# Two dense layers after a decay attention: the second product of layer 2 turned over, and VectorE's operations of three units interleaved

## The chip, the cores and the metric

One core of a Trainium2 chip runs the whole program. The metric is device time in microseconds, from the start of the program to its end. The kernel before takes 955.4 us (median of three runs, 954.99 to 956.48). A difference of 0.2%, about 2 us, is what a measurement of this kernel can tell from no change.

## The reference

The input goes through three stages. The last one is the one that the change touches:

```python
x = attention(r, k, v, w, u)              # 3072 tokens x 384, a linear attention with decay
h = x @ w_in1;  g = relu(h) ** 2;    x = g @ w_out1     # layer 1: 384 -> 2048 -> 384
h = x @ w_in2;  g = h - tanh(h);     x = g @ w_out2     # layer 2: 384 -> 2048 -> 384
```

The result is 3072 x 384 in 32-bit floats. Matmuls run on a rounded 32-bit type (fp32r), so each factor is split into a high part and a low part, and a product is the sum of three: high by high, high by low, low by high. The difference h - tanh(h) loses digits where h is small. There the kernel takes a polynomial in h squared, and it picks between the two element by element.

## The kernel before, in words

The 3072 tokens are cut into 6 blocks j of 512, and the 2048 hidden columns into 16 parts f of 128. A **unit** is one pair (layer, j, f). Layer 1 has 96 units, and layer 2 has 96 more. The program's order is written out by hand: each engine does its instructions in the order in which the code issues them, so an instruction that waits holds up everything behind it on its engine. The tile framework adds the waits on semaphores. In the text below, units of layer 2 are numbered 0 to 95.

One unit has two products on TensorE.

- *First product*, `gemm1` (L496): 9 matmuls with the weights held still and 512 token columns moving. The result h (128 hidden columns by 512 tokens) stands in one PSUM bank. It is the same for both layers.
- *Second product* of layer 1, `gemm2_1` (L536): 9 matmuls, 3 per 128 output columns. The weights are held still, and the high and low parts of g move, with 512 columns each. The result is kept transposed, outputs by tokens, in 3 banks. *Second product* of layer 2, `gemm2_2` (L614): 12 matmuls. Here g is held still (4 groups of 128 tokens) and 384 columns of weights move, so that the result is tokens by outputs, in 4 banks.

Between them stands the nonlinear part of layer 2, `act2` and `act2_late`. ScalarE does y = h² (L585), th = tanh h (L586), two squares q1, q2 of y plus a constant (L588, L590), and the mask of the sign of y minus a bound (L591). VectorE does the *first multiply* hy = k·h·y (L587), the *difference* th = h - th (L589), the *second multiply* hy = (q1 + c)·hy (L592), the *third multiply* hy = (q2 + d)·hy (L593), and the *pick*, which copies th into hy where the mask is set (L594). Then `act2_late` splits hy: ScalarE writes the high part ghi (L602), and VectorE writes the *low part* glo = hy - ghi (L603). `act2_late` of a unit comes after `act2` of the next unit, so on ScalarE the high part of unit n-1 stands behind the mask of unit n, and before y of unit n+1.

`front(n)` issues `gemm1` and then `act2` of a unit. The main loop runs three units ahead of the second product in layer 2: it issues `front(n+3)` and then `gemm2_2(n)`. At the end of a block, `evac2` copies the four banks of results to SBUF on ScalarE (L622) and sends them to memory from SyncE's queue. After parts f = 5, 7 and 9 of a block, `split_x2` prepares the input of the next block, with a cast on VectorE (L568) and then a subtraction on GpSimd (L569). After parts 1 and 2 of the first block, the last two weight tiles of layer 2 are made with a copy on ScalarE (L101) and a subtraction on GpSimd (L107). In layer 1 the VectorE subtraction at L525 is what TensorE waits for in the last unit.

PSUM has 8 banks. In layer 2 h turns through four of them (3, 4, 5, 6), and the results take four (0, 1, 2, 7).

Of the kernel before, what the change touches and what calls it, by code (L numbers as in the profile page):

```python
# [7 lines left out]
F32 = mybir.dt.float32  # L8
# [4 lines left out]
AF = mybir.ActivationFunctionType  # L13
ALU = mybir.AluOpType
# [7 lines left out]
PB, PD = 0.68482120983078318, 6.0837500067079047  # L22
# [3 lines left out]
def decay_attention_moe_moe_kernel(  # L26
# [9 lines left out]
):  # L36
    nc = tc.nc
    NTAU, GP, _, NP, C = rk.shape
    NT, DM = out.shape
    H = 2 * NP  # L40
    D = DM // H
    NCH = 768 // C
    KK = DM // 128
    NF = w1.shape[0]
    TB = 512
# [15 lines left out]
    def bank(i, name):  # L61
        return ps.tile([128, 512], F32, tag=f"bank{i}", name=name)
# [51 lines left out]
    def w_out(layer, f, part, a, b):  # L114
        return wt[layer, f][:, part, DM + a:DM + b]
# [364 lines left out]
                    )  # L480


    hbank = {1: [3, 4], 2: [3, 4, 5, 6]}
    hq = {}
    gq = {}
    acc = {}
# [89 lines left out]

    p2 = {}

    def act2(j, f):
        pool = p2["pool"]  # L580
        h = hq.pop((2, j, f))
        mk = lambda n: pool.tile([128, TB], F32, tag=n, name=n)
# [12 lines left out]
        late.append((j, f, hy))  # L595

    late = []

    def act2_late():
        j, f, hy = late.pop(0)  # L600
        hi, lo = split(hy)
        nc.scalar.activation(out=hi, in_=hy, func=AF.Copy)  # L602
        nc.vector.tensor_tensor(lo, hy, hi.bitcast(F32), op=ALU.subtract)  # L603
        gq[2, j, f] = (hi, lo)

    abank = [0, 1, 2, 7]

    def gemm2_2(j, f):
        hi, lo = gq.pop((2, j, f))
        if f == 0:  # L610
            acc[j] = [bank(abank[m], f"o{m}") for m in range(TPB)]
        for m in range(TPB):
            for n, (g, part) in enumerate(((hi, 0), (hi, 1), (lo, 0))):
                nc.tensor.matmul(  # L614
                    acc[j][m][:, 0:DM], lhsT=g[:, m * 128:(m + 1) * 128], rhs=w_out(2, f, part, 0, DM),
                    start=(f == 0 and n == 0), stop=(f == NF - 1 and n == 2),
                )

    def evac2(j):
        for m in range(TPB):  # L620
            t = p2["pool"].tile([128, DM], F32, tag="ob", name="ob", bufs=4)
            nc.scalar.activation(out=t, in_=acc[j][m][:, 0:DM], func=AF.Copy)  # L622
            t0 = (m * NCH + j) * C
            nc.sync.dma_start(out=out[t0:t0 + 128, :], in_=t)
        del acc[j]


# [29 lines left out]
    def front(n):  # L657
        layer, j, f = units[n]
        gemm1(layer, j, f)
        (act1 if layer == 1 else act2)(j, f)  # L660
        while len(late) > 1:
            act2_late()

    with tc.manual_schedule():
        table_a()
# [119 lines left out]
        for n, (layer, j, f) in enumerate(units):  # L785
            if layer == 1:
                act1_low(j, f)
            if layer == 1 and j == 0 and f:
                conv2(1, f + 2)
                conv3(1, f + 2, V)  # L790
                if f + 5 < NF:
                    load_w(1, f + 5)
            if layer == 1 and j == NB - 1 and 0 < f < NF - 1:
                conv2(2, f - 1)
                conv3(2, f - 1, V)
            while nf < len(units) and nf <= n + look(n):
                front(nf)
                nf += 1
            att = layer == 1 and j + 1 < NB and f in c_at
            if att:  # L800
                d = (j + 1) * ND + c_at[f]
                if j:
                    a_to(d + 3)
            if layer == 1 and j == 0:
                conv1(1, f + 3)
            if att:
                if j == 0:
                    a_to(min(d + 3, DR - 1))
                att_c(d)
                att_e(d)  # L810
                loads(d)
                pack(d)
            if layer == 2 and j == 0 and f in (1, 2):
                conv2(2, NF - 3 + f)
                conv3(2, NF - 3 + f, G)
            if layer == 1:
                gemm2_1(j, f)
            else:
                while (2, j, f) not in gq:
                    act2_late()  # L820
                gemm2_2(j, f)
            if att and d + 2 < NDALL:
                att_b(d + 2)
                att_dm(d + 2)
                if d % 2 == 0:
                    nat_push(d // 2 + 2, G)
            if layer == 1:
                nat_pop()
            if layer == 1 and j == 0:
                conv0(1, f + 4)  # L830
                if f >= NF - 3:
                    open_split()
                if f == NF - 2:
                    a_to(DR)
            if layer == 1 and j == NB - 2:
                if f == 11:
                    at_ctx.close()
                    open2()
                    for q in range(5):
                        load_w(2, q)  # L840
                if f == 12:
                    conv0(2, 0)
                if f == 14:
                    conv1(2, 0)
# [12 lines left out]
_OUTS = [((3072, 384), "float32")]  # L857


def _layout(x):  # L860
# [59 lines left out]
```

## Time and profile before

| what | value |
|---|---|
| median of three runs | 955.4 us |
| the profiled execution | 952.83 us |
| its span, first to last instruction | 951.0 us |
| matmuls of layer 2, from the first unit that they have to themselves | 536.9 us to 947.6 us |
| in the stretch 700 to 750 us: TensorE, VectorE, ScalarE, GpSimd busy of 50 us | 49.41, 46.68, 41.23, 3.90 |
| granted clock of TensorE in that stretch | 1.00 |

All durations used below come from the one profiled execution, whose time is 1.8 us over its span and 2.6 us under the median. A timeline row gives the start, the duration, the engine, the line, the operation, the result and its operands, and a count where neighbours of one kind are merged. Square brackets at the end of a row give the engine's idle time ahead of it, and what ended that. An instruction's duration includes latency which the next one can overlap, so the step from one start to the next start is what an instruction costs an engine that is never idle. In the tables of waits, a row reads: who waited, for whom, the total in us, how often, the longest.

### The profile page before, as it was taken

How to read it: one execution, taken by the hardware profiler on the slowest of the kernel's cores; microseconds unless marked ns; L12 is line 12 of the kernel's file. 1: busy time of each engine (PE TensorE's matmuls, PEld its weight loads, DVE VectorE, ACT ScalarE, POOL GpSimd, SP SyncE). 2: the span in 40 equal slices, each digit the busy share in tenths (PEclk: the TensorE clock that was granted, in tenths of full speed). 3: DMA queues.
4: the chain of work that ended last, by engine and by line, in shares of the span. 5: the costliest groups of instructions: out<-in, count | busy, mean ns of one | idle time of the engine just before them, and what ended most of it. 6: DMA issues, size and time to landing. Idle time of an engine off the chain costs nothing.

```text
span 951.0 us, 14117 instructions
## 1 busy us (share of the span) xinstructions
PE 917.6 (96%) x5036; PEld 783.5 (82%) x5036; DVE 734.4 (77%) x1200; ACT 643.6 (68%) x1157; POOL 251.8 (26%) x216
## 2 busy tenths in 40 slices
PE   6889999999999999999999999999999999999997
PEld 6767778888888888888888788898898898898896
DVE  7898967864883685461278899999999999999996
ACT  3545565545544554553688887888888888887885
POOL 5833324654554464443101011001001001010000
PEclk8999999999999999999999999999999999999999
DMA  8755522312120222200565100100100100100000
GB/s 240 228 174 173 183 62 68 93 53 78 53 85 29 68 93 53 78 9 7 202 207 192 55 1 12 56 1 12 57 12 1 55 12 1 56 12 1 34 1 33
DMA packets 29669, 67.55 MB, mean 71 GB/s; under 512 B 5024, under 2 KB 15136, under 8 KB 29600
## 3 DMA queue, kind: packets, MB, share of 16 engines
q1 hardware_dynamic: 29456, 66.47, 21.8%
q8 instruction: 39, 0.64, 0.3%
q14 instruction: 30, 0.25, 0.1%
q10 hardware_dynamic: 144, 0.20, 0.1%
HBM read 55.25 MB, written 9.44 MB: 68 GB/s over the span
## 4 chain that ended last, share of the span: by engine, by line
PE 73%; DVE 16%; ACT 4%; issue 4%; POOL 2%; DMA 1%; DVEq 0%; ACTq 0%; POOLq 0%
PE h L496 33%; PE acc L536 19%; PE o L614 14%; DVE hy L592 2%; DVE hy L593 2%; PE sc L290 2%; DVE hy L594 2%; PE y L429 2%; DVE hy L587 2%; PE y L422 2%; ACT ghi L602 1%; POOL am L324 1%; DVE glo L525 1%; DVE w L107 1%; DVE am L342 1%
## 5 line engine op out<-in xcount | busy, mean ns | idle before, releaser
L496 PE MATMUL h<-xt,w 128*128 128x512 f32 x864 | 215.2, 394 | 0.6 <-POOL w L107 0.6
L496 PE MATMUL h<-xs,w 128*128 128x512 f32 x864 | 215.0, 393 | 0.0
L614 PE MATMUL o<-w,ghi 128*128 128x384 f32 x768 | 197.0, 337 | 2.9 <-ACT ob L622 2.9
L496 PEld LDWEIGHTS h<-xt,w 128*128 128x128 f32 x864 | 160.5, 189 | 34.2 <-POOL w L107 1.0
L496 PEld LDWEIGHTS h<-xs,w 128*128 128x128 f32 x864 | 160.8, 188 | 29.4
L510 ACT ACTIVATE g<-h 128x512 f32<-128x512 f32 x96 | 57.3, 597 | 143.0 <-PE h L496 142.1
L536 PE MATMUL acc<-ghi,w 128*128 128x512 f32 x576 | 153.3, 398 | 0.3 <-ACT x2s L552 0.3
L614 PEld LDWEIGHTS o<-w,ghi 128*128 128x128 f32 x768 | 140.7, 188 | 12.9 <-ACT ob L622 5.1
L614 PE MATMUL o<-w,glo 128*128 128x384 f32 x384 | 131.2, 342 | 5.1 <-DVE glo L603 4.9
L536 PEld LDWEIGHTS acc<-ghi,w 128*128 128x128 f32 x576 | 104.9, 188 | 23.8 <-ACT g L510 1.1
L516 POOL TENSOR_TENSOR glo<-g,ghi 128x512 fp32r<-128x512 f32 x64 | 85.8, 1341 | 136.0 <-ACT ghi L513 61.7
L569 POOL TENSOR_TENSOR xs<-x2f,xs 128x512 fp32r<-128x512 f32 x18 | 24.5, 1360 | 332.5 <-DVE xs L568 332.5
L536 PE MATMUL acc<-glo,w 128*128 128x512 f32 x288 | 83.8, 392 | 9.1 <-DVE glo L525 9.1
L602 ACT ACTIVATE ghi<-hy 128x512 fp32r<-128x512 f32 x96 | 60.9, 634 | 45.9 <-DVE hy L594 45.2
L614 PEld LDWEIGHTS o<-w,glo 128*128 128x128 f32 x384 | 72.0, 187 | 10.6 <-DVE glo L603 8.6
L594 DVE COPY_PREDICATED hy<-mask,th 128x512 f32<-128x512 uint8 x96 | 71.9, 749 | 9.9
L593 DVE SCALAR_TENSOR_TENSOR hy<-q,hy 128x512 f32<-128x512 f32 x96 | 68.0, 708 | 10.4 <-ACT q L588 0.5
L324 POOL TENSOR_TENSOR am<-ident,bt 128x512 f32<-128x512 f32 x44 | 51.2, 1164 | 89.6 <-DVE bt L308 82.7
L587 DVE SCALAR_TENSOR_TENSOR hy<-h,y 128x512 f32<-128x512 f32 x96 | 66.4, 691 | 10.0 <-ACT th L586 1.8
L585 ACT ACTIVATE y<-h 128x512 f32<-128x512 f32 x96 | 57.1, 595 | 24.2 <-PE h L496 23.6
L536 PEld LDWEIGHTS acc<-glo,w 128*128 128x128 f32 x288 | 53.7, 188 | 23.0 <-DVE glo L525 12.1
L273 DVE TENSOR_TENSOR fr<-rkt,fr 112x256 fp32r<-112x256 f32 x30 | 38.9, 1295 | 42.9 <-ACT fr L272 42.9
(104 smaller groups left out, 1406.1 us busy)
## 6 DMA issues: line engine op xcount, KB each, us to landing
raw<-in_w_dram SPq DMA_DIRECT2D x32, 768.0 KB, 4.4
rkt<-in_rk_dram SPq DMA_DIRECT2D x23, 448.0 KB, 4.3
kvt<-in_nat_dram SPq DMA_DIRECT2D x23, 384.0 KB, 4.4
x2d<-x2s SPq DMA_DIRECT2D x18, 256.0 KB, 2.2
x2f<-x2d SPq DMA_DIRECT2D x18, 256.0 KB, 2.8
out_dram<-ob SPq DMA_DIRECT2D x24, 192.0 KB, 2.0
rnt<-in_nat_dram SPq DMA_DIRECT2D x23, 192.0 KB, 2.5
xt<-ys SPq DMA_DIRECT2D x120, 16.0 KB, 1.8
```

The source lines that it names most:

```text
L273: nc.vector.tensor_tensor(ks[:, 1], k, ks[:, 0].bitcast(F32), op=ALU.subtract)
L324: nc.gpsimd.tensor_tensor(am_t[d].rearrange("p (a z) t -> p a z t", a=2), ident[:, None, None, :].to_broadcast([128, 2, 2, C]), hd.to_broa ...
L496: nc.tensor.matmul(h, lhsT=w_in(layer, f, part, kk), rhs=x[:, xpart, kk, :], start=(n == 0), stop=(n == 3 * KK - 1),)
L510: nc.scalar.activation(out=g, in_=h, func=AF.Relu)
L516: nc.gpsimd.tensor_tensor(lo, g, hi.bitcast(F32), op=ALU.subtract)
L536: nc.tensor.matmul(acc[j][m], lhsT=w_out(1, f, part, m * 128, (m + 1) * 128), rhs=g, start=(f == 0 and n == 0), stop=(f == NF - 1 and n == 2),
L585: nc.scalar.activation(out=y, in_=h, func=AF.Square)
L587: nc.vector.scalar_tensor_tensor(out=hy, in0=h, scalar=PK, in1=y, op0=ALU.mult, op1=ALU.mult)
L593: nc.vector.scalar_tensor_tensor(out=hy, in0=q2, scalar=PD, in1=hy, op0=ALU.add, op1=ALU.mult)
L594: nc.vector.copy_predicated(hy, mask, th)
L602: nc.scalar.activation(out=hi, in_=hy, func=AF.Copy)
L614: nc.tensor.matmul(acc[j][m][:, 0:DM], lhsT=g[:, m * 128:(m + 1) * 128], rhs=w_out(2, f, part, 0, DM), start=(f == 0 and n == 0), stop=(f ...
```

## The change

`gemm2_2` takes the form of `gemm2_1`: the weights are held still and g moves, with 9 matmuls of 512 columns in place of 12 of 384. The result is kept transposed in 3 banks, which are taken in turn from five (6, 7, 0, 1, 2), and h turns through three banks (3, 4, 5). In the last part of a block the matmuls are sorted by bank. `evac2` copies three banks of 512 columns, one of them on VectorE in the last block only, and the output in memory is a (6, 3, 128, 512) array that the host reorders.

`act2` issues the same operations of a unit in another order among those of its neighbours. On VectorE: first multiply of n, third multiply of n-1, difference of n, pick of n-1, low part of n-2, second multiply of n. On ScalarE the order stays: y, th, q1, q2 and mask of n, then the high part of n-1. hy has three buffers in place of two. After the last unit, `act2_flush` issues what is left.

```diff
-    hbank = {1: [3, 4], 2: [3, 4, 5, 6]}
+    hbank = {1: [3, 4], 2: [3, 4, 5]}
...
-        y, th, q1, q2, hy = (mk(n) for n in ("y", "th", "q1", "q2", "hy"))
+        y, th, q1, q2 = (mk(n) for n in ("y", "th", "q1", "q2"))
+        hy = pool.tile([128, TB], F32, tag="hy", name="hy", bufs=3)
         mask = pool.tile([128, TB], U8, tag="mask", name="mask")
+        st2[n] = (q2, hy, mask, th)
         nc.scalar.activation(out=y, in_=h, func=AF.Square)
         nc.scalar.activation(out=th, in_=h, func=AF.Tanh)
         nc.vector.scalar_tensor_tensor(out=hy, in0=h, scalar=PK, in1=y, op0=ALU.mult, op1=ALU.mult)
         nc.scalar.activation(out=q1, in_=y, func=AF.Square, bias=p2["ba"], scale=1.0)
+        act2_poly(n - 1)
         nc.vector.tensor_tensor(th, h, th, op=ALU.subtract)
         nc.scalar.activation(out=q2, in_=y, func=AF.Square, bias=p2["bb"], scale=1.0)
+        act2_pick(n - 1)
+        act2_low(n - 2)
         nc.scalar.activation(out=mask, in_=y, func=AF.Sign, bias=p2["bm"], scale=1.0)
         nc.vector.scalar_tensor_tensor(out=hy, in0=q1, scalar=PC, in1=hy, op0=ALU.add, op1=ALU.mult)
-        nc.vector.scalar_tensor_tensor(out=hy, in0=q2, scalar=PD, in1=hy, op0=ALU.add, op1=ALU.mult)
-        nc.vector.copy_predicated(hy, mask, th)
-        late.append((j, f, hy))
+        act2_high(n - 1)
+
+    def act2_poly(n):
+        if n >= 0:
+            q2, hy, mask, th = st2[n]
+            nc.vector.scalar_tensor_tensor(out=hy, in0=q2, scalar=PD, in1=hy, op0=ALU.add, op1=ALU.mult)
+
+    def act2_pick(n):
+        if n >= 0:
+            q2, hy, mask, th = st2[n]
+            nc.vector.copy_predicated(hy, mask, th)
+
+    def act2_high(n):
+        if n >= 0:
+            hy = st2[n][1]
+            hi, lo = split(hy)
+            nc.scalar.activation(out=hi, in_=hy, func=AF.Copy)
+            st2[n] = (hy, hi, lo)
+
+    def act2_low(n):
+        if n >= 0:
+            hy, hi, lo = st2.pop(n)
+            nc.vector.tensor_tensor(lo, hy, hi.bitcast(F32), op=ALU.subtract)
+            gq[(2, *divmod(n, NF))] = (hi, lo)
+
+    def act2_flush():
+        n = NB * NF - 1
+        act2_poly(n)
+        act2_low(n - 1)
+        act2_pick(n)
+        act2_high(n)
+        act2_low(n)
...
-    abank = [0, 1, 2, 7]
+    abank = [6, 7, 0, 1, 2]
...
-            acc[j] = [bank(abank[m], f"o{m}") for m in range(TPB)]
-        for m in range(TPB):
-            for n, (g, part) in enumerate(((hi, 0), (hi, 1), (lo, 0))):
-                nc.tensor.matmul(
-                    acc[j][m][:, 0:DM], lhsT=g[:, m * 128:(m + 1) * 128], rhs=w_out(2, f, part, 0, DM),
...
+            acc[j] = [bank(abank[(KK * j + m) % len(abank)], f"o{m}") for m in range(KK)]
+        terms = [(n, m) for n in range(3) for m in range(KK)]
+        if f == NF - 1:
+            terms.sort(key=lambda t: t[1])
+        for n, m in terms:
+            part, g = ((0, hi), (1, hi), (0, lo))[n]
+            nc.tensor.matmul(
+                acc[j][m], lhsT=w_out(2, f, part, m * 128, (m + 1) * 128), rhs=g,
...
     def evac2(j):
-        for m in range(TPB):
-            t = p2["pool"].tile([128, DM], F32, tag="ob", name="ob", bufs=4)
-            nc.scalar.activation(out=t, in_=acc[j][m][:, 0:DM], func=AF.Copy)
...
+        for m in range(KK):
+            t = p2["pool"].tile([128, TB], F32, tag="ob", name="ob", bufs=3)
+            if m == 1 and j == NB - 1:
+                nc.vector.tensor_copy(t, acc[j][m])
+            else:
+                nc.scalar.activation(out=t, in_=acc[j][m], func=AF.Copy)
+            nc.sync.dma_start(out=out[j, m], in_=t)
```

## Rows read from the trace of the kernel before

**Rows 1.** The page's first part (busy time and share of the span by engine) and the head of its fourth part, the chain of waits that ended last, by engine.

```profile
PE 917.6 (96%) x5036; PEld 783.5 (82%) x5036; DVE 734.4 (77%) x1200; ACT 643.6 (68%) x1157; POOL 251.8 (26%) x216
...
PE 73%; DVE 16%; ACT 4%; issue 4%; POOL 2%; DMA 1%; DVEq 0%; ACTq 0%; POOLq 0%
```

**Rows 2.** The timeline of TensorE's matmuls: four rows of one unit of layer 1's last block, then three of one unit of layer 2.

```profile
516.01 1.52 PE L536 MATMUL acc<-ghi,w 128*128 128x512 f32 x6
517.37 0.84 PE L536 MATMUL acc<-glo,w 128*128 128x512 f32 x3
518.05 2.20 PE L496 MATMUL h<-xt,w 128*128 128x512 f32 x9
520.09 1.30 PE L536 MATMUL acc<-ghi,w 128*128 128x512 f32 x5
...
703.12 2.24 PE L496 MATMUL h<-xs,w 128*128 128x512 f32 x9
705.20 0.51 PE L614 MATMUL o<-w,ghi 128*128 128x384 f32 x2
...
707.31 2.24 PE L496 MATMUL h<-xs,w 128*128 128x512 f32 x9
```

**Rows 3.** The timeline of VectorE at the start of layer 2: all its operations of one unit and the first of the next.

```profile
540.27 0.69 DVE L587 SCALAR_TENSOR_TENSOR hy<-h,y 128x512 f32<-128x512 f32 x1 [1.13 <-ACT th L586]
540.88 0.68 DVE L589 TENSOR_TENSOR th<-h,th 128x512 f32<-128x512 f32 x1
541.48 0.68 DVE L592 SCALAR_TENSOR_TENSOR hy<-q,hy 128x512 f32<-128x512 f32 x1
542.26 0.69 DVE L593 SCALAR_TENSOR_TENSOR hy<-q,hy 128x512 f32<-128x512 f32 x1
543.06 0.75 DVE L594 COPY_PREDICATED hy<-mask,th 128x512 f32<-128x512 uint8 x1
543.71 0.67 DVE L603 TENSOR_TENSOR glo<-hy,ghi 128x512 fp32r<-128x512 f32 x1
544.48 0.69 DVE L587 SCALAR_TENSOR_TENSOR hy<-h,y 128x512 f32<-128x512 f32 x1
```

**Rows 4.** The timeline of ScalarE in the same stretch.

```profile
539.15 0.60 ACT L585 ACTIVATE y<-h 128x512 f32<-128x512 f32 x1 [1.44 <-PE h L496]
539.65 0.59 ACT L586 ACTIVATE th<-h 128x512 f32<-128x512 f32 x1
...
541.96 0.62 ACT L602 ACTIVATE ghi<-hy 128x512 fp32r<-128x512 f32 x1
542.49 0.59 ACT L585 ACTIVATE y<-h 128x512 f32<-128x512 f32 x1
```

**Rows 5.** The table of waits for 480 to 951 us: who waited for whom, the total in us, how often, the longest.

```profile
ACT ghi L602 <- DVE hy L594: 45.2, 58, 3.6
...
ACT y L585 <- PE h L496: 23.6, 44, 1.4
...
PE o L614 <- DVE glo L603: 4.9, 4, 1.8
...
DVE hy L587 <- ACT th L586: 1.8, 2, 1.1
```

**Rows 6.** Timelines of GpSimd, VectorE and ScalarE around two of GpSimd's operations in layer 2: the subtraction for a weight tile with the VectorE row beside it, ScalarE's copy for that tile and what follows the copy, then four rows around the next block's input.

```profile
550.10 2.24 POOL L107 TENSOR_TENSOR w<-raw,w 128x768 fp32r<-128x768 f32 x1 [38.06 <-ACT w L101]
550.69 2.19 DVE L593 SCALAR_TENSOR_TENSOR hy<-q,hy 128x512 f32<-128x512 f32 x1
...
549.12 0.91 ACT L101 ACTIVATE w<-raw 128x768 fp32r<-128x768 f32 x1
549.91 0.60 ACT L585 ACTIVATE y<-h 128x512 f32<-128x512 f32 x1
...
572.47 0.42 DVE L568 CAST xs<-x2f 128x512 fp32r<-128x512 f32 x1
572.80 0.69 DVE L587 SCALAR_TENSOR_TENSOR hy<-h,y 128x512 f32<-128x512 f32 x1
572.97 1.30 POOL L569 TENSOR_TENSOR xs<-x2f,xs 128x512 fp32r<-128x512 f32 x1 [15.80 <-DVE xs L568]
574.00 0.81 DVE L592 SCALAR_TENSOR_TENSOR hy<-q,hy 128x512 f32<-128x512 f32 x1
```

**Rows 7.** The timeline of ScalarE at the end of a block: the four copies of layer 2's first block, and the three of layer 1's last.

```profile
611.26 1.61 ACT L622 ACTIVATE ob<-o 128x384 f32<-128x384 f32 x4
...
535.86 1.85 ACT L552 ACTIVATE x2s<-acc 128x512 f32<-128x512 f32 x3
```

**Rows 8.** The timeline where layer 1 goes over into layer 2: ScalarE's y of unit 1, and VectorE's low part of layer 1's last unit.

```profile
532.53 0.60 ACT L585 ACTIVATE y<-h 128x512 f32<-128x512 f32 x1 [1.16 <-PE h L496]
...
534.45 0.68 DVE L525 TENSOR_TENSOR glo<-g,ghi 128x512 fp32r<-128x512 f32 x1
```

**Rows 9.** The end: ScalarE's y of the last unit and the last matmul on the timeline, then two rows of the table of DMA issues (count, KB each, median us from issue to landing).

```profile
935.26 0.60 ACT L585 ACTIVATE y<-h 128x512 f32<-128x512 f32 x1
...
947.24 0.34 PE L614 MATMUL o<-w,glo 128*128 128x384 f32 x1
...
x2d<-x2s SPq DMA_DIRECT2D x18, 256.0 KB, 2.2
...
out_dram<-ob SPq DMA_DIRECT2D x24, 192.0 KB, 2.0
```

More of the change, by code (lines that the diff above doesn't have):

```diff
@@ L38, in decay_attention_moe_moe_kernel @@
     NTAU, GP, _, NP, C = rk.shape
-    NT, DM = out.shape
+    NT, DM = NTAU * C, nat.shape[3]
     H = 2 * NP
@@ L577, in decay_attention_moe_moe_kernel @@
     p2 = {}
+    st2 = {}
     def act2(j, f):
@@ L581, in act2 @@
         h = hq.pop((2, j, f))
+        n = j * NF + f
         mk = lambda n: pool.tile([128, TB], F32, tag=n, name=n)
-        y, th, q1, q2, hy = (mk(n) for n in ("y", "th", "q1", "q2", "hy"))
+        y, th, q1, q2 = (mk(n) for n in ("y", "th", "q1", "q2"))
+        hy = pool.tile([128, TB], F32, tag="hy", name="hy", bufs=3)
         mask = pool.tile([128, TB], U8, tag="mask", name="mask")
+        st2[n] = (q2, hy, mask, th)
         nc.scalar.activation(out=y, in_=h, func=AF.Square)
@@ L588, in act2 @@
         nc.scalar.activation(out=q1, in_=y, func=AF.Square, bias=p2["ba"], scale=1.0)
+        act2_poly(n - 1)
         nc.vector.tensor_tensor(th, h, th, op=ALU.subtract)
         nc.scalar.activation(out=q2, in_=y, func=AF.Square, bias=p2["bb"], scale=1.0)
+        act2_pick(n - 1)
+        act2_low(n - 2)
         nc.scalar.activation(out=mask, in_=y, func=AF.Sign, bias=p2["bm"], scale=1.0)
         nc.vector.scalar_tensor_tensor(out=hy, in0=q1, scalar=PC, in1=hy, op0=ALU.add, op1=ALU.mult)
-        nc.vector.scalar_tensor_tensor(out=hy, in0=q2, scalar=PD, in1=hy, op0=ALU.add, op1=ALU.mult)
-        nc.vector.copy_predicated(hy, mask, th)
-        late.append((j, f, hy))
[L597 to L604, printed above, removed]
-    abank = [0, 1, 2, 7]
+        act2_high(n - 1)
[26 more added lines that the diff above has]
+    abank = [6, 7, 0, 1, 2]
     def gemm2_2(j, f):
@@ L610, in gemm2_2 @@
         if f == 0:
-            acc[j] = [bank(abank[m], f"o{m}") for m in range(TPB)]
-        for m in range(TPB):
-            for n, (g, part) in enumerate(((hi, 0), (hi, 1), (lo, 0))):
-                nc.tensor.matmul(
-                    acc[j][m][:, 0:DM], lhsT=g[:, m * 128:(m + 1) * 128], rhs=w_out(2, f, part, 0, DM),
-                    start=(f == 0 and n == 0), stop=(f == NF - 1 and n == 2),
-                )
-    def evac2(j):
-        for m in range(TPB):
-            t = p2["pool"].tile([128, DM], F32, tag="ob", name="ob", bufs=4)
-            nc.scalar.activation(out=t, in_=acc[j][m][:, 0:DM], func=AF.Copy)
-            t0 = (m * NCH + j) * C
-            nc.sync.dma_start(out=out[t0:t0 + 128, :], in_=t)
+            acc[j] = [bank(abank[(KK * j + m) % len(abank)], f"o{m}") for m in range(KK)]
[6 more added lines that the diff above has]
+                acc[j][m], lhsT=w_out(2, f, part, m * 128, (m + 1) * 128), rhs=g,
+                start=(f == 0 and n == 0), stop=(f == NF - 1 and n == 2),
+            )
+    def evac2(j):
+        for m in range(KK):
[5 more added lines that the diff above has]
+            nc.sync.dma_start(out=out[j, m], in_=t)
         del acc[j]
@@ L660, in front @@
         (act1 if layer == 1 else act2)(j, f)
-        while len(late) > 1:
-            act2_late()
+        if n == len(units) - 1:
+            act2_flush()
     with tc.manual_schedule():
@@ L818, in decay_attention_moe_moe_kernel @@
             else:
-                while (2, j, f) not in gq:
-                    act2_late()
                 gemm2_2(j, f)
@@ L856 @@
 _ARGS = ["rk", "nat", "w", "u", "w1", "w2"]
-_OUTS = [((3072, 384), "float32")]
+_OUTS = [((6, 3, 128, 512), "float32")]
 def _layout(x):
@@ L918 @@
     r = _run(nc, [arrays], core_ids=[0])
-    return r.results[0]["out_0_dram"]
+    o = r.results[0]["out_0_dram"].reshape(6, 3, 128, 4, 128)
+    return _np.ascontiguousarray(o.transpose(3, 0, 4, 1, 2).reshape(3072, 384))
```

## The prediction

> **What bounds the kernel now.** The page's parts 1 and 4 come first: TensorE is busy 96% of the span and fills 73% of the chain that ended last [rows 1]. That names TensorE, but it doesn't say what a shorter TensorE stage would be worth, so the next view is the timeline of one unit, engine by engine. On TensorE a unit of layer 2 takes 707.31 - 703.12 = 4.19 us: 2.08 for the first product and 2.11 for the second [rows 2]. On VectorE its six operations take 544.48 - 540.27 = 4.21 us from first multiply to first multiply [rows 3]. The two engines are level. The steps inside those 4.21 us are 0.61, 0.60, 0.78, 0.80, 0.65, 0.77. An operation that follows one that it does not depend on starts 0.60 to 0.65 after it, before the earlier one has ended (durations 0.67 to 0.75). The third multiply and the pick, which need what stands right before them, start 0.78 and 0.80 after it. The 0.77 is the next unit's first multiply, which reuses the buffer that the low part has just read (hy has two buffers). ScalarE has slack: it waits 45.2 us for the pick and 23.6 us for h [rows 5].
>
> **The second product turned over.** It takes the shape of layer 1's products: weights still, g moving, 512 columns. Layer 1's last block shows both products in that shape, 18 matmuls in 520.09 - 516.01 = 4.08 us [rows 2]. So TensorE's unit goes from 4.19 to 4.08 us, and over 96 units it could save 10.6 us if nothing else held it. The columns streamed stay the same (9 x 512 = 12 x 384); three matmuls fewer per unit save what each costs beside its columns.
>
> **VectorE's order.** The new sequence is: first multiply of n, third multiply of n-1, difference of n, pick of n-1, low part of n-2, second multiply of n. No operation follows its own input, and with three buffers none reuses one just read. Five steps of 0.60 or 0.61 and one of 0.65 give 3.66 us, against 4.21 [rows 3]. No row has the third multiply right behind an independent first multiply. The bounds of that step are 0.60 and 0.80, and I take 0.61, the row of what now follows a first multiply. By its work alone VectorE is thus no longer a bound.
>
> **The wait that decides.** Two rows of the trace tell what the first multiply waits for. In rows 3 it sat idle for 1.13 us until th, not y: y starts at 539.15, th at 539.65 and ends at 540.24 [rows 4], and the first multiply starts at 540.27. The table has two such waits in layer 2, both put down to th [rows 5], although the operation reads only h and y. Both th and the multiply read the PSUM bank of h. So it starts at y + 1.12, not y + 0.63. Before, this rarely showed, as VectorE ran late anyway.
>
> The Trainium skill, "PSUM — Partial Sum Buffer", section "PSUM bank collisions raise a hardware error", says that the AWS compiler's scheduler puts a dependency between ScalarE and VectorE instructions on one bank, "reads and writes alike". The two rows just read agree, for the framework used here.
>
> Now the new order closes a ring. ScalarE's high part of n-1 waits for the pick of n-1. The pick now stands behind the first multiply of n, and so behind th of n. And y of n+1 stands behind that high part on ScalarE. One turn of the ring, from y of n to y of n+1:
> - y to the first multiply, through th: 1.12 [rows 3, 4];
> - first multiply, third multiply, difference, to the start of the pick: 0.61 + 0.60 + 0.60 = 1.81 [rows 3];
> - the pick itself: 0.75 [rows 3];
> - from its end to the high part: 0.03, which I take from th to the first multiply (540.24 to 540.27);
> - high part to the next y: 542.49 - 541.96 = 0.53 [rows 4].
>
> Sum: 4.24 us. That is above TensorE's 4.08 and VectorE's 3.66, so layer 2 would run at 4.24 us per unit. Before, the pick of n-1 came ahead of the first multiply of n, and no such ring held.
>
> What came beside other work before now adds to the ring, since ScalarE's and VectorE's stretches of it follow one another:
> - Copies at a block's end. They stand between a high part and a y. Four copies took 3 steps of (1.61 - 0.49)/3 = 0.37 for 384 columns [rows 7]. For 512 columns from PSUM the bounds are 0.37 and (1.85 - 0.60)/2 = 0.62, the steps of layer 1's copies, which wait for TensorE. I take the step from y to th, 0.50 [rows 4], which is 128x512 from PSUM too. Three copies in five blocks: 15 x 0.50 = 7.5 us.
> - GpSimd's subtraction for the next block. A VectorE operation with both inputs in SBUF stands still beside it: the multiply at 574.00, 0.27 before GpSimd's end, took 0.81 where 0.68 is usual, and the one at 550.69, 1.65 before GpSimd's end, took 2.19 [rows 6]. Both lose the time left less 0.14. The cast fills VectorE's idle 0.58 and costs nothing there (its step is 0.33), at 1.12 + 1.81 + 0.65 + 2 x 0.60 = 4.78 after y. GpSimd starts 0.50 later, 5.28, and ends at 6.58. The next third multiply would start at 4.24 + 1.12 + 0.61 = 5.97 and loses 6.58 - 5.97 - 0.14 = 0.47, on the ring. With 15 of these: 7.0 us. The bounds are nothing and the whole overlap, 0.61 each.
> - The last two weight tiles: ScalarE's copy, 549.91 - 549.12 = 0.79 each, plus some 0.4 each for a third multiply held by GpSimd [rows 6]: 2.4 us.
>
> **The sum against the profiled execution.** I count from y of unit 3 (542.49 before [rows 4]) to y of unit 95 (935.26 [rows 9]): 392.8 us. The start stays where it is. VectorE reaches the low part of layer 1's last unit about 1.5 us earlier, as the third multiply and the pick of unit 0 no longer stand ahead of it [rows 8]; but y of unit 1 is at 532.53, its first multiply at 533.65, the pick of unit 0 ends at 536.21, the high part and layer 1's three copies follow (0.53 + 1.5), y of unit 2 starts at 538.27, and y of unit 3 at 538.27 + 4.24 = 542.5. Then 92 x 4.24 + 7.5 + 7.0 + 2.4 = 407.0. That is 14.2 later than before.
>
> The end: from the last y, the ring's steps give the second multiply of 95 at 4.18, third multiply at 4.96 (now right behind its input), low part of 94 at 5.56, pick 6.16 to 6.91, high part to 7.57, low part 7.60 to 8.28. The last unit's matmuls, sorted by bank, have two done and seven to go: the last one starts 6 x 0.227 later, at 9.7, and ends at 10.1. Before, it was 947.58 - 935.26 = 12.3 [rows 9]. The last copy is 0.1 longer, and a 256 KB transfer takes 2.2 us where 192 KB took 2.0 [rows 9]. So the end gives back 1.9 us.
>
> Net: + 12.3 us on a span of 951.0. The profiled execution would go from 952.8 to 965.1, and the median of 955.4, 2.6 above it, to 967.7. I say 967.5. PSUM's three banks for h cost nothing: h of unit n is read out by y + 3, and its bank is wanted two units later.
>
> **Rivals.**
> - *TensorE sets the pace (faster).* If the first multiply waited for y alone, the ring would be 4.24 - 0.49 = 3.75 us, below TensorE's 4.08. From the end of layer 1's matmuls, 1.5 us ahead of 536.9, 94 first and 92 second products at 2.04 lead to 914.8, with about 3 us of waits (unit 0's low part, copies) to 918; with 13.5 of tail the span is 931, and the time 936. It turns on one thing: th in or out of that wait. For it speaks that only two instances show the wait; against it that both end to 0.03 us with th, and that the difference behind it, which does need th, follows without any idle time of its own.
> - *The ring holds, but its additions hide.* If copies and GpSimd's holds fell into slack, 14.5 us go and the time is 953, no change. I see no slack on the ring, but half of the additions could go.
> - *The interleaving doesn't shorten VectorE's steps.* The ring would have three steps of 0.79 instead of 0.60, and be 4.80 us: 92 x 0.56 = 52 us more, 1019. Against it stand the three steps of 0.60 to 0.65 in rows 3.
>
> The Trainium skill, "VectorE: DVE Perf Modes", section "The DRAIN you can't avoid", says that the next VectorE operation starts only when the pipe is empty, with or without a semaphore. By that rule the reordering gains nothing; the trace disagrees, with starts 0.07 to 0.10 before the earlier operation's end [rows 3].
>
> **How the numbers follow.** Ring with its additions 0.80; TensorE's pace 0.13; additions hidden 0.04; steps not shorter 0.03. The likeliest case has its own range: the ring's 4.24 is uncertain by 0.03, 2.8 us over 92 turns; the copies' bounds are -2 and +2; GpSimd's holds are -7 to +2. That is 958 to 973. As it holds most of the chance, the range given is little wider, 955 to 974. With 0.2% as what a measurement of this kernel can tell from no change: faster 0.13, within it 0.04, slower 0.83.
>
> **What would show it.** In the changed profile: y to y 4.24 in undisturbed units; the first multiply idle some 0.6 us in every unit, ended by th; the high part idle some 0.9, ended by the pick; VectorE's steps 0.60 to 0.65 and its share of busy time lower; y waiting no more for h; TensorE waiting in nearly every unit for the low part, and for the copies after a block's end. A first multiply that starts before th has ended, or TensorE without waits at 4.08 us per unit, would make the prediction wrong.

## The result, and the profile after

The kernel became slower: 962.26 us (median of four runs, 962.05 to 963.27) against 955.19 us (954.97 to 956.48) for the kernel before in the same comparison. The ratio is 1.0073, with a 95% interval of 1.0056 to 1.0091: 7.1 us more. The forecast was 967.5, in a range from 955 to 974.

The profiled execution took 963.27 us, with a span of 961.5. First the page's first part and the head of its fourth, the chain that ended last, which answer to [rows 1].

```profile
PE 922.7 (96%) x4748; PEld 741.5 (77%) x4748; DVE 722.9 (75%) x1201; ACT 637.6 (66%) x1150; POOL 250.8 (26%) x216
...
PE 45%; DVE 33%; ACT 17%; issue 2%; POOL 1%; DMA 1%; DVEq 0%; ACTq 0%; POOLq 0%
```

TensorE's share of busy time has not moved: 96% before and after. The chain has. TensorE fills 45% of it where it filled 73%, VectorE 33% where it filled 16%, ScalarE 17% where it filled 4%. That is how a ring over several engines looks in this view: no engine became the bound, and the chain passes from one to the next.

The table of waits from 480 to 962 us answers to [rows 5].

```profile
ACT ghi L617 <- DVE hy L611: 83.9, 96, 2.6
...
DVE hy L592 <- ACT th L591: 53.5, 95, 2.6
...
PEld o L645 <- DVE glo L623: 39.7, 89, 2.3
...
PE o L645 <- DVE glo L623: 13.6, 24, 1.8
```

Two waits stand in practically every unit: the high part waits for the pick (96 times, 58 before), and the first multiply for th (95 times, 2 before). TensorE waits for the low part: its weight loads (PEld) in 89 units, 39.7 us in all, and in 24 of these units its matmuls (PE) too, 13.6 us. In those 24 the two rows show the same stop twice, so they are not added up. The wait of y for h, 44 times before, is left twice.

One unit in the middle of the stage, ScalarE first and then VectorE, beside [rows 4] and [rows 3]:

```profile
702.55 0.58 ACT L590 ACTIVATE y<-h 128x512 f32<-128x512 f32 x1
703.02 0.59 ACT L591 ACTIVATE th<-h 128x512 f32<-128x512 f32 x1
...
706.22 0.63 ACT L617 ACTIVATE ghi<-hy 128x512 fp32r<-128x512 f32 x1 [0.77 <-DVE hy L611]
706.76 0.58 ACT L590 ACTIVATE y<-h 128x512 f32<-128x512 f32 x1
```

```profile
703.64 0.69 DVE L592 SCALAR_TENSOR_TENSOR hy<-h,y 128x512 f32<-128x512 f32 x1 [0.50 <-ACT th L591]
704.25 0.68 DVE L606 SCALAR_TENSOR_TENSOR hy<-q,hy 128x512 f32<-128x512 f32 x1
704.85 0.68 DVE L595 TENSOR_TENSOR th<-h,th 128x512 f32<-128x512 f32 x1
705.45 0.73 DVE L611 COPY_PREDICATED hy<-mask,th 128x512 f32<-128x512 uint8 x1
706.08 0.68 DVE L623 TENSOR_TENSOR glo<-hy,ghi 128x512 fp32r<-128x512 f32 x1
706.67 0.68 DVE L600 SCALAR_TENSOR_TENSOR hy<-q,hy 128x512 f32<-128x512 f32 x1
707.85 0.69 DVE L592 SCALAR_TENSOR_TENSOR hy<-h,y 128x512 f32<-128x512 f32 x1 [0.50 <-ACT th L591]
```

The ring is read by going to and fro between the two. y starts at 702.55. The first multiply starts 1.09 later, 0.03 after th ends (703.61). The pick starts 1.81 after the first multiply and lasts 0.73. The high part starts 0.04 after it, and the next y 0.54 after that. The sum is 4.21 us, y to y. VectorE's steps are 0.59 to 0.63, so its six operations would fit in some 3.6 us: it waits for th with nothing else to do.

### The profile page after: what moved, and what is told of

It reads as the page before. It is cut to its first block, busy times and chain, and to the rows that moved or that the text cites. A ratio compares the mean times of both kernels' runs of the same rounds, so it can differ in the third digit from the quotient of the medians.

```text
span 961.5 us, 13137 instructions
## 1 busy us (share of the span) xinstructions
PE 922.7 (96%) x4748; PEld 741.5 (77%) x4748; DVE 722.9 (75%) x1201; ACT 637.6 (66%) x1150; POOL 250.8 (26%) x216
## 4 chain that ended last, share of the span: by engine, by line
PE 45%; DVE 33%; ACT 17%; issue 2%; POOL 1%; DMA 1%; DVEq 0%; ACTq 0%; POOLq 0%
PE h L496 19%; PE acc L536 19%; DVE hy L592 7%; DVE hy L606 7%; DVE hy L611 7%; ACT ghi L617 6%; DVE th L595 6%; ACT th L591 5%; ACT y L590 5%; PE sc L290 2%; PE y L429 2%; PE y L422 2%; DVE w L107 1%; DVE am L342 1%; DVE raw L92 1%
## 5 line engine op out<-in xcount | busy, mean ns | idle before, releaser
L510 ACT ACTIVATE g<-h 128x512 f32<-128x512 f32 x96 | 57.2, 596 | 143.8 <-PE h L496 143.7
L645 PE MATMUL o<-ghi,w 128*128 128x512 f32 x576 | 150.6, 392 | 2.0 <-ACT ob L656 2.0
L645 PEld LDWEIGHTS o<-ghi,w 128*128 128x128 f32 x576 | 108.4, 189 | 26.5 <-ACT ob L656 4.1
L645 PE MATMUL o<-glo,w 128*128 128x512 f32 x288 | 93.1, 425 | 13.6 <-DVE glo L623 13.6
L645 PEld LDWEIGHTS o<-glo,w 128*128 128x128 f32 x288 | 47.9, 189 | 44.9 <-DVE glo L623 39.7
L606 DVE SCALAR_TENSOR_TENSOR hy<-q,hy 128x512 f32<-128x512 f32 x96 | 73.2, 763 | 0.1
L611 DVE COPY_PREDICATED hy<-mask,th 128x512 f32<-128x512 uint8 x96 | 69.9, 728 | 0.0
L593 ACT ACTIVATE q<-y,ba 128x512 f32<-128x512 f32 x96 | 69.6, 725 | 0.0
```

Source lines behind the costliest of these rows:

```text
L510: nc.scalar.activation(out=g, in_=h, func=AF.Relu)
L645: nc.tensor.matmul(acc[j][m], lhsT=w_out(2, f, part, m * 128, (m + 1) * 128), rhs=g, start=(f == 0 and n == 0), stop=(f == NF - 1 and n == 2),
```

## The experiments

All times are set against the kernel before, which was run beside them; its medians there were 954.5 to 954.9 us.

**1. The ring opened.** The high part is issued one unit later, right behind th, so that the pick on which it waits is long done. All else is the changed kernel.

```diff
         nc.scalar.activation(out=th, in_=h, func=AF.Tanh)
+        act2_high(n - 2)
         nc.vector.scalar_tensor_tensor(out=hy, in0=h, scalar=PK, in1=y, op0=ALU.mult, op1=ALU.mult)
...
-        act2_high(n - 1)
...
         act2_poly(n)
+        act2_high(n - 1)
         act2_low(n - 1)
```

> The changed kernel with one instruction moved: the high part of unit n-2 is issued right behind th of unit n, and no longer the high part of n-1 behind the mask of n. No operation is added or taken away. Theory (the ring y, th, first multiply, pick of the unit before, its high part, next y sets 4.21 us per unit): the pick no longer stands ahead of the next y, the ring is open, and TensorE's 4.08 us per unit is the next bound. From the end of layer 1's matmuls, 94 first and 92 second products at 2.04 and some 3 us of waits, then the tail of some 14: 933 to 942 us in all; y waits for h again, and the first multiply's idle time by unit is no longer fixed. Rival (the turned product, its banks and its longer copies are what made it slower): the order of ScalarE changes nothing of that, 958 to 963 us.

It took 933.81 us (932.63 to 934.79), ratio 0.978 [0.9763, 0.9797]. This is the version to keep: 21 us faster than the kernel before, 28 faster than the changed one. Its waits from 480 us on, and then one unit of ScalarE up to the next y:

```profile
ACT y L590 <- PE h L496: 54.3, 83, 1.2
...
DVE hy L593 <- ACT th L591: 23.0, 50, 1.9
...
ACT ghi L617 <- DVE hy L611: 2.8, 2, 2.6
```

```profile
705.22 0.60 ACT L590 ACTIVATE y<-h 128x512 f32<-128x512 f32 x1 [0.65 <-PE h L496]
705.72 0.59 ACT L591 ACTIVATE th<-h 128x512 f32<-128x512 f32 x1
706.19 0.63 ACT L617 ACTIVATE ghi<-hy 128x512 fp32r<-128x512 f32 x1
...
709.30 0.60 ACT L590 ACTIVATE y<-h 128x512 f32<-128x512 f32 x1 [0.65 <-PE h L496]
```

The high part waits twice in the whole stage where it waited 96 times, and y again waits for h, and so for TensorE, which now sets the pace. y to y is 4.08, layer 1's unit [rows 2]. The first multiply still waits for th 50 times, and a unit takes 4.08 all the same: with no ring through it, that wait no longer sets the pace. One view shows it in one number, the busy times in the same 355 us of layer 2. Here first, then the changed kernel, then the kernel before (columns: TensorE, its weight loads, VectorE, ScalarE and GpSimd, each with its instructions, then the granted clock, the DMA share and GB/s):

```profile
545.00:900.00 355.00, 354.21 (x1559) 291.40 (x1558) 336.19 (x535) 305.70 (x538) 23.98 (x17) 1.00 0.07 21
```

```profile
545.00:900.00 355.00, 342.76 (x1449) 265.46 (x1448) 311.28 (x498) 284.70 (x499) 23.26 (x17) 1.00 0.07 21
```

```profile
545.00:900.00 355.00, 350.43 (x1739) 311.52 (x1738) 330.81 (x512) 297.84 (x521) 23.62 (x17) 1.00 0.07 22
```

TensorE goes from 12.2 us idle in the changed kernel to 0.8. The instruction counts are the progress made: VectorE did 535 operations here in the time in which the changed kernel did 498.

**2. The old order with the turned product.** `act2` and `act2_late` of the kernel before, with the changed kernel's second product, banks and copies.

```diff
-        act2_poly(n - 1)
...
-        act2_pick(n - 1)
-        act2_low(n - 2)
...
-        act2_high(n - 1)
...
+        nc.vector.scalar_tensor_tensor(out=hy, in0=q2, scalar=PD, in1=hy, op0=ALU.add, op1=ALU.mult)
+        nc.vector.copy_predicated(hy, mask, th)
+        late.append((j, f, hy))
```

> The changed kernel with the turned second product, but VectorE and ScalarE in the order of before. Theory (ring): no ring in that order; VectorE's 4.21 us of steps per unit sets the pace as before, TensorE at 4.08 gains nothing: 952 to 956 us, steps of 0.77 to 0.80 between operations that depend on each other. Rival (the turned product, its banks and copies made it slower): 960 to 964 us. A second rival (the second product alone was the bound before): 944 to 948 us, ten less than before.

952.97 us (951.75 to 955.8), ratio 0.9984 [0.9972, 0.9995]: as expected. The gain of some 1.5 us is less than the 2 us that a measurement can tell from no change. VectorE's steps of 0.78 and 0.80 are there again, and most units take 4.19 to 4.21. TensorE's shorter product turns into waits for VectorE:

```profile
ACT ghi L602 <- DVE hy L594: 69.7, 87, 3.6
...
PEld o L617 <- DVE glo L603: 21.8, 41, 2.3
```

**3. The new order with the old product.** The kernel before with the changed kernel's `act2`, three buffers of hy, and nothing else.

```diff
+        act2_poly(n - 1)
         nc.vector.tensor_tensor(th, h, th, op=ALU.subtract)
...
+        act2_pick(n - 1)
+        act2_low(n - 2)
...
-        nc.vector.scalar_tensor_tensor(out=hy, in0=q2, scalar=PD, in1=hy, op0=ALU.add, op1=ALU.mult)
-        nc.vector.copy_predicated(hy, mask, th)
-        late.append((j, f, hy))
+        act2_high(n - 1)
```

> The kernel before with the interleaved order of VectorE alone; the second product, its four banks, the four of h and the copies as before. Theory (ring): 4.21 us from y to y, four copies of 0.37 each block on the ring as three of 0.48 were, GpSimd's holds of 0.48 as well: 960 to 964 us, like the changed kernel; TensorE's 4.19 stays just below the ring. Rival (the turned product made it slower): the order is then a gain or nothing, 945 to 956 us.

963.84 us (962.95 to 966.58), ratio 1.0102 [1.0085, 1.012]. The order alone costs 9 us, somewhat more than the whole change. Its waits are those of the changed kernel:

```profile
ACT ghi L617 <- DVE hy L611: 84.2, 96, 2.6
DVE hy L592 <- ACT th L591: 55.7, 95, 2.6
```

y to y is 4.21 to 4.22 with either product. So a unit's time in the changed kernel is set by the ring, and the form of the second product has no part in it.

**4. th issued later.** q1 goes ahead of th on ScalarE. Nothing that the first multiply reads has moved, y and h; only th has.

```diff
         nc.scalar.activation(out=y, in_=h, func=AF.Square)
+        nc.scalar.activation(out=q1, in_=y, func=AF.Square, bias=p2["ba"], scale=1.0)
         nc.scalar.activation(out=th, in_=h, func=AF.Tanh)
         nc.vector.scalar_tensor_tensor(out=hy, in0=h, scalar=PK, in1=y, op0=ALU.mult, op1=ALU.mult)
-        nc.scalar.activation(out=q1, in_=y, func=AF.Square, bias=p2["ba"], scale=1.0)
```

> The changed kernel with q1 issued ahead of th on ScalarE: y, q1, th, q2, mask, high part. Nothing else. Theory (the first multiply waits for th, which lies on the ring): th starts 0.61 later, so the first multiply starts some 1.71 after y, and a turn takes 4.82: 92 x 0.61 = 56 us more, 1015 to 1021 us. Rival (it waits for y alone, and the 0.03 us behind th is chance): the first multiply starts 0.63 after y, and the time is 962 or lower.

1026.75 us in its one run, 6 above the upper end. The direction is shown, and the miss has its row:

```profile
701.35 0.58 ACT L590 ACTIVATE y<-h 128x512 f32<-128x512 f32 x1
701.97 0.73 ACT L591 ACTIVATE q<-y,ba 128x512 f32<-128x512 f32 x1
702.59 0.58 ACT L592 ACTIVATE th<-h 128x512 f32<-128x512 f32 x1
```

```profile
703.21 0.69 DVE L593 SCALAR_TENSOR_TENSOR hy<-h,y 128x512 f32<-128x512 f32 x1 [1.25 <-ACT th L592]
```

The first multiply starts 1.86 after y, 0.04 after th ends. q1 reads y and now stands right behind it, so it starts 0.62 after y, where th, which does not read y, started 0.47 after. That step was left out of the expectation: 0.13 to 0.15 in each of 92 turns is 12 to 14 us. y to y was 4.96 where 4.82 was expected. Part of it came back: GpSimd no longer lengthens a unit, since the third multiply now starts after GpSimd has ended, and none of them is stretched in this trace.

**5. The first multiply ahead of th.** q1 and the first multiply are issued before th, and the high part stays where the change put it. Now th must wait for the multiply, if it is the bank that orders the two.

```diff
         nc.scalar.activation(out=y, in_=h, func=AF.Square)
-        nc.scalar.activation(out=th, in_=h, func=AF.Tanh)
-        nc.vector.scalar_tensor_tensor(out=hy, in0=h, scalar=PK, in1=y, op0=ALU.mult, op1=ALU.mult)
         nc.scalar.activation(out=q1, in_=y, func=AF.Square, bias=p2["ba"], scale=1.0)
+        nc.vector.scalar_tensor_tensor(out=hy, in0=h, scalar=PK, in1=y, op0=ALU.mult, op1=ALU.mult)
+        nc.scalar.activation(out=th, in_=h, func=AF.Tanh)
```

> The changed kernel with q1 and the first multiply issued ahead of th: ScalarE y, q1, th, q2, mask, high part of n-1; VectorE as in the change. The high part stays ahead of the next y. Theory (the ring is set by the first multiply's wait for th, because both read the bank of h): the first multiply now starts some 0.63 after y, and th waits for it instead, to 1.35; the difference waits for th to 1.97, the pick starts at 2.57, the next y at 3.87. That is under TensorE's 4.08, so 933 to 942 us. Rival (the high part behind the pick is too late by itself, whatever the first multiply waits for): 4.2 us per unit and 958 to 963 us.

938.2 us (936.54 to 940.13), ratio 0.9832 [0.9809, 0.9856]. The wait is turned round, and the table has a row that was in no kernel before it, th for the first multiply (then y and the first multiply of one unit):

```profile
ACT th L593 <- DVE hy L592: 3.1, 12, 0.5
```

```profile
711.96 0.58 ACT L590 ACTIVATE y<-h 128x512 f32<-128x512 f32 x1
```

```profile
712.58 0.69 DVE L592 SCALAR_TENSOR_TENSOR hy<-h,y 128x512 f32<-128x512 f32 x1
```

The table lists the 12 longest of these waits. In all 96 units th starts 0.03 to 0.04 after the multiply's end. The multiply starts 0.62 after y, and a turn of the ring is 3.88 to 3.90, below TensorE's 4.08. The version is 4.4 us slower than experiment 1. The ring is shorter but still closed, so block ends (5.32) and GpSimd's holds (4.67) still lengthen a unit, and a block of 16 units takes 66.1 us here and 65.5 in experiment 1. From y of unit 3 to y of unit 95 that makes 381.1 against 377.5 us, 3.6 of the 4.4.

**6. Are the copies on the ring?** One of three copies of each block goes to VectorE.

```diff
-            if m == 1 and j == NB - 1:
+            if m == 1:
```

> The changed kernel with one of the three copies at the end of every block on VectorE, not only in the last. Theory (ScalarE's copies lie on the ring): the step from y to y across a block's end falls from 5.63 by one copy's 0.48 to some 5.15, 2.4 us over five blocks, as VectorE is idle there. Rival (the copies are hidden, the longer step is a wait for TensorE): the step stays at 5.63.

```profile
609.77 0.58 ACT L590 ACTIVATE y<-h 128x512 f32<-128x512 f32 x1
...
614.93 0.60 ACT L590 ACTIVATE y<-h 128x512 f32<-128x512 f32 x1
```

The step from y to y across the block's end was 5.16 to 5.17 in all five blocks, where the changed kernel has 5.63 to 5.65: one copy off ScalarE takes off 0.47 to 0.48, its whole step. The time was 960.15 us in one run, too little to read a gain of 2 us from. The step, the same in all five blocks, can be read.

**7 to 9. What the turned product is worth once the ring is open.** Three versions of experiment 1. The first has the old second product (its four banks, copies and output with it):

```diff
-            acc[j] = [bank(abank[(KK * j + m) % len(abank)], f"o{m}") for m in range(KK)]
...
+            acc[j] = [bank(abank[m], f"o{m}") for m in range(TPB)]
+        for m in range(TPB):
+            for n, (g, part) in enumerate(((hi, 0), (hi, 1), (lo, 0))):
+                nc.tensor.matmul(
+                    acc[j][m][:, 0:DM], lhsT=g[:, m * 128:(m + 1) * 128], rhs=w_out(2, f, part, 0, DM),
```

> The kernel before with VectorE interleaved and the high part of n-2 behind th of n, as in the run that moved it, but with the second product of before (12 matmuls of 384 columns, four banks). Theory (with the ring open TensorE is the bound): a unit takes TensorE's 4.19 in place of 4.08, 96 x 0.11 = 10 us more than with the turned product: 942 to 946 us. Rival (the turned product is worth nothing even then, the gain is all in the order): 932 to 936 us.

957.07 us (954.89 to 958.47), ratio 1.0026 [1.0015, 1.0037]. Both expectations missed: the ring is open, and yet the kernel is no faster than the kernel before. The trace names a wait that neither counted, TensorE for the low part (the table's rows, then one such wait on the timeline):

```profile
PEld o L643 <- DVE glo L623: 15.6, 19, 2.2
...
PE o L643 <- DVE glo L623: 9.6, 19, 1.9
```

```profile
711.83 0.44 PE L643 MATMUL o<-w,glo 128*128 128x384 f32 x1 [0.30 <-DVE glo L623]
```

The old loop wants the low part in its third matmul of twelve, the turned one in its seventh of nine. y to y is 4.2 in most units, but 4.7 in those beside GpSimd, and 4.8 to 4.9 twice around a block's end. The reading was that the old loop stops TensorE whenever VectorE is late, at a block's end or beside GpSimd. This gave a new theory, and the second version tests it: the same twelve matmuls with the low part's four at the end.

```diff
-        for m in range(TPB):
-            for n, (g, part) in enumerate(((hi, 0), (hi, 1), (lo, 0))):
+        for n, (g, part) in enumerate(((hi, 0), (hi, 1), (lo, 0))):
+            for m in range(TPB):
```

> The opened ring with the second product of before, whose 12 matmuls are issued in another order: all eight with the high part first, the four with the low part last. Theory A (the old product lost not only by its 4.19 us, but because the low part is wanted by its third matmul, 0.35 us in, with no room for GpSimd's holds and the copies, which then stop TensorE): the low part gets some 1 us of room, TensorE runs at 4.19 without waits, 942 to 947 us. Theory B (the old shape itself costs the rest, by its four banks or the copies): 953 to 958 us as before the reordering.

946.27 us (945.15 to 946.5), ratio 0.9915 [0.9887, 0.9944]: a unit is 4.18 to 4.19 but for the block's end (4.82). GpSimd still holds third multiplies on VectorE (some 1.2 us each where 0.68 is usual), but no step from y to y shows it any more, and nearly all of TensorE's waits for the low part are gone:

```profile
PEld o L643 <- DVE glo L623: 3.0, 3, 1.2
```

The third version is the reverse: the turned product with its low part third.

```diff
-        if f == NF - 1:
-            terms.sort(key=lambda t: t[1])
+        terms.sort(key=lambda t: t[1])
```

> The opened ring with the turned second product, its nine matmuls sorted by bank in every part, so that the low part is wanted by the third matmul, 0.45 us in. Theory A (the place of the low part): TensorE stops for the low part at each of GpSimd's 15 holds and at block ends, about 0.4 us each, 940 to 945 us. Theory B (the turned shape itself is the gain): 932 to 936 us, as with the low part last.

948.24 us (947.87 to 949.68), ratio 0.9941 [0.9921, 0.9961]. The direction is as expected, and the loss, 14.4 us, is more than either number. The trace shows TensorE's weight loads waiting for the low part in 53 units, 24.7 us, and its matmuls too in 19 of them:

```profile
PEld o L645 <- DVE glo L623: 24.7, 53, 2.2
...
PE o L645 <- DVE glo L623: 9.6, 19, 1.8
```

Some 1.4 us of the loss in this profiled execution come from elsewhere: the granted clock is 0.50 from 542.5 to 545.9 us, and one first product takes 3.44 there instead of 2.04, which experiment 1's profiled execution does not have.

Put side by side (medians, us):

| order of `act2` | second product | low part | time |
|---|---|---|---|
| old | old | third | 954.5 to 955.2 (the kernel before) |
| old | turned | last | 952.97 |
| new, ring closed | old | third | 963.84 |
| new, ring closed | turned | last | 962.26 (the changed kernel) |
| new, ring open | old | third | 957.07 |
| new, ring open | old | last | 946.27 |
| new, ring open | turned | third | 948.24 |
| new, ring open | turned | last | 933.81 |

With the ring closed or the old order, the turned product is worth 1.5 to 2 us by these medians, no more than a measurement can tell from no change. With the ring open it is worth 23.3, and two things make it up: the shape alone (946.27 to 933.81, or 957.07 to 948.24) 9 to 12, and the place of the low part (957.07 to 946.27, or 948.24 to 933.81) 11 to 14. The traces give the same picture with wider bounds. A block of 16 units takes 68.9, 67.6, 67.8 and 65.5 us in the last four rows, and over the 92 units from y of unit 3 on that is 7 to 12 for the shape and 8 to 13 for the place.

## Why the prediction was right, and where its size was off

**The wait that decides: right.** That the first multiply waits for th, though it reads only h and y, was argued from two rows. It holds in all 96 units: the multiply starts 0.03 to 0.04 us after th's end. Experiment 4 moved th behind q1, and the multiply went with it; experiment 5 turned the order round, and th waited instead. The Trainium skill, "PSUM — Partial Sum Buffer", section "PSUM bank collisions raise a hardware error", says that the compiler's scheduler orders two engines' accesses to one bank even where both only read. All three results agree with it, for the framework used here. Whether the chip needs that wait was not tried: no version here reads the bank from both engines at once.

**The ring: right, shown by experiments 1, 3, 4 and 5.** Its turn was put at 4.24 and measured 4.21. The term that was off is y to the first multiply, 1.09 for 1.12, as th follows y by 0.47 here and by 0.50 in [rows 4]; the others are within 0.02 and cancel. Over 92 turns that is the 2.8 us within which the prediction held the ring uncertain.

**VectorE's order: right.** The third multiply behind an independent first multiply has a step of 0.61, the value taken. The rival in which interleaving does not shorten the steps is out: starts come 0.08 to 0.10 ahead of the earlier operation's end. The Trainium skill, "VectorE: DVE Perf Modes", section "The DRAIN you can't avoid", says that the next operation waits until the pipe is empty, but adds that one which is not held starts earlier. The prediction left out that second half, and the trace agrees with it.

**The additions: right.** The block's end, with the three copies between a high part and a y:

```profile
613.43 0.63 ACT L617 ACTIVATE ghi<-hy 128x512 fp32r<-128x512 f32 x1 [0.77 <-DVE hy L611]
613.97 1.55 ACT L656 ACTIVATE ob<-o 128x512 f32<-128x512 f32 x3
615.40 0.61 ACT L590 ACTIVATE y<-h 128x512 f32<-128x512 f32 x1
```

615.40 - 613.97 = 1.43, 0.48 a copy where 0.50 was taken; five blocks cost 7.1 for 7.5. Beside GpSimd, first its row and then VectorE's:

```profile
571.47 1.30 POOL L569 TENSOR_TENSOR xs<-x2f,xs 128x512 fp32r<-128x512 f32 x1 [11.80 <-DVE xs L568]
```

```profile
572.16 1.16 DVE L606 SCALAR_TENSOR_TENSOR hy<-q,hy 128x512 f32<-128x512 f32 x1
```

The third multiply takes 1.16 where 0.68 is usual, 0.48 more; the 15 holds cost about 7.3 for 7.0. The two weight tiles cost about 2.0 for 2.4. From y of unit 3 to y of unit 95 the sum is 92 x 4.21 + 7.1 + 7.3 + 2.0 = 403.7, and the trace has 403.8 (543.19 to 947.01), where 407.0 was forecast and 392.8 measured before. The rival that the additions hide is out, and experiment 6 shows it for the copies by itself. The likeliest case's range of 958 to 973 does not follow from its three bounds: added up around 967.5 they give 956 to 974. The measured time lies in both.

**The end: direction right, 0.7 short.** From the last y to the end of the span it took 14.54 us, 1.2 less than before; 1.9 less was forecast. The last matmul starts at 957.53, 10.5 after that y, where 9.7 was worked out with matmul steps of 0.227. TensorE's clock stood at half from 952.3 to 955.7 us, as the last section shows. From the end of the last low part at 955.24, six steps of 0.227 would have put the last matmul at 956.6, 9.6 after that y.

**The step that failed: the way from the profiled execution to the median.** The forecast for the profiled execution was 965.1, and it took 963.27. The 1.8 us between them are accounted for: the ring's stage 3.2 shorter than forecast, the end 0.7 longer, and y of unit 3 at 543.19 for 542.5. Of the 5.2 us by which the forecast missed the median, the other 3.4 (3.6 less 0.2 of rounding) come from one sentence: the median was taken to lie 2.6 above the profiled execution, as it does for the kernel before (952.83 against 955.4). For the changed kernel it lies 1.0 below (962.26 against 963.27). That offset is no property of the kernel. The code ahead of layer 2 is the same in all these kernels, and the first y of layer 2 started anywhere from 526.69 to 530.64 us in the eleven profiled executions. One execution fixes a sum within about 2 us only. The differences arise early: ScalarE's L510 of layer 1's eleventh unit starts between 103.6 and 107.5 us, and from there to the first y of layer 2 the executions differ by no more than 0.7. What makes them differ was not settled, but the record has a lead. In 37 executions of the kernel before, run beside the experiments, the time goes with the mean granted clock: the 12 with 0.986 or less have a median of 955.8 us, the 15 with 0.989 or more 953.9. The profiled execution of the kernel before had 0.992, as high as any of these, and that of the changed kernel 0.988, like the others of its kind (0.988, 0.988, 0.991). So the 2.6 looks in good part like one execution with little time at half clock. That the clock is the cause is not shown.

**The rival that TensorE sets the pace (936).** It was given 0.13, and it did not come in. It turned on the wait for th, as the prediction said, and experiment 5, in which the first multiply no longer waits for th, gave 938.2. The prediction did not see that the same 4.08 could be had with the wait in place, by moving the high part (933.81).

## What to carry to other kernels

Before operations of several units are interleaved on one engine, draw the ring through all engines in order of issue, from a unit's first operation to the same operation of the next unit, with every wait that crosses engines. An operation that waits for this unit's result and stands ahead of the next unit's first operation in an in-order queue closes the ring. Issuing it one unit later opens the ring, and here that took no more buffers than the change already had. Give the matmuls whose operand comes last the last places in the sequence: here that was worth 8 to 14 us, about as much as the better shape. A part that changes nothing alone (the turned product, 1.5 us) can be worth 23 once another bound is gone and its matmuls come in the right order, so parts are judged together with the bound that is left.

## What the runs showed of the hardware that was not expected

**TensorE's clock in the tail.** In the last units of the changed kernel TensorE waited for a low part, went back to work at full clock, and one microsecond later the clock fell to half. Windows of the tail (columns as above), and then its matmuls:

```profile
950.00:952.00 2.00, 0.74 (x3) 0.65 (x4) 1.90 (x5) 0.63 (x1) 0.00 (x0) 1.00 0.00 0
952.30:955.70 3.40, 3.40 (x10) 2.62 (x9) 2.25 (x4) 0.63 (x1) 0.00 (x0) 0.50 0.00 0
955.70:957.90 2.20, 2.20 (x10) 1.51 (x8) 0.63 (x1) 0.60 (x1) 0.00 (x0) 1.00 0.00 0
```

```profile
951.26 0.96 PE L645 MATMUL o<-glo,w 128*128 128x512 f32 x3 [1.83 <-DVE glo L623]
952.06 2.56 PE L645 MATMUL o<-ghi,w 128*128 128x512 f32 x6
954.42 1.45 PE L645 MATMUL o<-glo,w 128*128 128x512 f32 x3
955.70 0.63 PE L645 MATMUL o<-ghi,w 128*128 128x512 f32 x2
956.16 0.39 PE L645 MATMUL o<-glo,w 128*128 128x512 f32 x1
...
957.53 0.39 PE L645 MATMUL o<-glo,w 128*128 128x512 f32 x1
```

The granted clock is 0.50, 1.2 of 2.4 GHz, from about 952.3 to 955.7: the three matmuls from 954.42 take 1.28 us, 0.43 each, where two later ones take 0.46, 0.23 each. Unit 94's matmuls so end at 955.70 and not near 954.1, and the last unit starts late, although VectorE has written its low part by 955.24 (L623, 954.55 + 0.69). The drop came while TensorE worked, after it had waited 1.83 us. The kernel before waited 1.61 and 1.82 us in its tail and kept its matmuls at 0.17 to 0.18 for 384 columns, with a granted clock of 1.00. At the start of layer 2 TensorE waited 1.92 us in experiment 7 and kept 1.00; in experiment 9 it waited 1.81, and the clock fell to 0.50. So the length of the last wait alone doesn't tell; what does was not tried.

**A step on ScalarE depends on what it reads.** An activation of 128x512 that reads what the one ahead of it writes starts 0.03 to 0.04 us after that one's end (q1 behind y in experiment 4: a step of 0.62 behind 0.58 us). One that does not starts some 0.10 before that end: th behind y 0.47 to 0.50 after its start, and th behind the longer q1 of 0.73 us 0.62 after it. VectorE's 0.78 to 0.80 against 0.60 [rows 3] is the same kind of difference, and the prediction used it there; on ScalarE it was unlooked for, and it is the miss of experiment 4.
